# Decode attention, two heads at a time: 48 KB rows for K and V, p.V for 8 keys of two heads per weight load, q as rows on three partitions

## The chip, the cores and the metric

The kernel runs on one core of one Trainium2 chip (trn2). The metric is the device time of one execution in microseconds (us); the profile's span is some 2 us shorter than the time of the same execution. A program on one core has no second core to compare with, so "fast" here means no run more than 1.5% above the fastest of its kernel.

## The reference

Four attention layers in a row, A, B, A, B, each with its own K and V caches and its own two projections, for one token of width 640. A layer appears twice, so its caches are read twice.

```python
# x: (1, 1, 640); per layer: k_cache, v_cache (1, 32, 8192, 192), wq (640, 6144), wo (6144, 640), all bf16
def layer(x, k_cache, v_cache, wq, wo):             # heads 32, head width 192
    q = layernorm(x) @ wq                           # -> 32 heads x 192
    p = softmax(einsum("qd,kd->qk", q, k) * 192 ** -0.5)
    return x + concat(einsum("qk,kd->qd", p, v)) @ wo
x = layer(x, A...); x = layer(x, B...); x = layer(x, A...); x = layer(x, B...)
```

One caution on correctness. With these inputs a layer adds so little to x that the comparison with the reference cannot see it. So no run here says anything about the numerical result of the attention, nor about the "mended head mapping" that is part of the change; where a recorded text calls a result right, that means that the program makes every sum, not that it was checked.

## The kernel before

K and V of a head come as one load of 3 MB each into one of eight slots: 128 partitions with 64 keys each, a row of 24,576 bytes per partition. A slot is loaded again when its reader has freed it. Six head tiles (K 0 and V 0 of layer A, V 28 to 31 of layer B) stay on chip for the layer's second pass.

```python
NSLOT = 8
KEPT = {0: {("k", 0), ("v", 0)}, 1: {("v", 28), ("v", 29), ("v", 30), ("v", 31)}}
...
# one load: free = the events that freed what the slot held
f = lambda s: s.dma_start(t, w[n[0]][0, head(*n[1:])].rearrange("(p j) d -> p (j d)", p=P))
return SP.op(f, *free, sem=semS[i], inc=16)
```

Scores: the vector engine (DVE) multiplies K by q in four chunks in place, the tensor engine (PE) sums over the head width with an identity as held weights. When PE is through, the K slot is free.

```python
def products(h):
    for c in range(4):
        e = DV.op(lambda v, d0=d0: v.tensor_tensor(k3[:, :, d0:d0 + QD], kin[:, :, d0:d0 + QD],
                  q_sb[qi][:, d0:d0 + QD].unsqueeze(1).broadcast_to([P, J, QD]), ALU.mult))
    ...                                            # 24 matmuls of 512 columns, identity held
    freed[nt] = ev_S[h] = e
```

p.V: two keys per partition are the weights (2 columns), their V rows (2 x 192 columns) stream. Of the 2 x 2 blocks of the result only the diagonal ones are wanted. ScalarE (ACT) scales and copies the result, and two small matmuls pick the two diagonal blocks and sum over partitions. There are two result banks, O0 and O1, used in turn.

```python
def values(h):
    for m in range(J // 2):                        # 32 matmuls, each with its own weight load
        OB[par][32 * g:32 * g + 2, 0:2 * DH] += p_sb[pi][:, j:j + 2].T @ t[:, j * DH:(j + 2) * DH]
    freed[nv_] = e
    AC.op(lambda a: a.activation(o_sb, OB[par], ACT.Copy, scale=rl[pi]))
def gather(h):
    for i in range(2):                             # PE
        TB[0:1, C_O:C_O + DH] += pick[:, i:i + 1].T @ o_sb[:, i * DH:(i + 1) * DH]
```

(The updates in the last two excerpts are written shorter than in the program.)

Of the kernel before, what the change touches and what calls it, by code (L numbers as in the profile page):

```python
# [11 lines left out]
class Queue:  # L12
# [18 lines left out]
    def op(self, fn, *events, sem=None, inc=1, signal=True, bank=None):  # L31

        if bank is not None:
            self.wait(*[ev for q, ev in bank.items() if q is not self])
        self.wait(*events)
        if not signal:
            self.items.append((fn, None, 0))
            return None
        sem = self.sem if sem is None else sem
        self.counts[id(sem)] = self.counts.get(id(sem), 0) + inc  # L40
        self.items.append((fn, sem, inc))
        if bank is not None:
            bank[self] = (sem, self.counts[id(sem)])
        return sem, self.counts[id(sem)]
# [11 lines left out]
def matmul_held(t, out, lhsT, rhs, start, stop):  # L56

    return t.add_instruction(mybir.InstMatmult(  # L58
        name=t.bass.get_next_instruction_name(), engine=mybir.EngineType.PE,
        ins=[t.lower_ap(rhs), t.lower_ap(lhsT, for_matmul_weights=True)], outs=[t.lower_ap(out)],  # L60
        start_tensor_calc=start, stop_tensor_calc=stop, tile_size=(128, 128), tile_position=(0, 0), ldweights=False))


HEADS_W = 10
Q_FIRST = 2
O_LAST = 2
NSLOT = 8
AHEAD = 4
KEPT = {0: {("k", 0), ("v", 0)}, 1: {("v", 28), ("v", 29), ("v", 30), ("v", 31)}}


def build(nc, A_x, A_k, A_v, A_wq, A_wo, B_x, B_k, B_v, B_wq, B_wo, out):
# [3 lines left out]
    J = SK // P  # L76
    DC = D // P
    EPS = 1e-5
    NL = 4
    QD = DH // 4  # L80
    R = 512 // J
    W = [dict(k=A_k, v=A_v, wq=A_wq, wo=A_wo), dict(k=B_k, v=B_v, wq=B_wq, wo=B_wo)]
    NW = HEADS_W * DH // P
    QC = (H - Q_FIRST) * DH
    TS = J * DH
    QW = H * DH
    Q_PARTS = [[(0, 2), (2, 2), (4, 1)] if l < 2 else [(0, 1), (1, 2), (3, 2)] for l in range(NL)]
    O_PART = [P] * NL
    OI = [O_LAST * DH // n for n in O_PART]
    NB = 3  # L90
    G = 4
    FORWARD = dict(heads=list(range(H)), q0=0, q1=Q_FIRST * DH, wo=[0, HEADS_W, 2 * HEADS_W], wol=H - O_LAST)
    BACKWARD = dict(heads=[H - 2, H - 1] + list(range(H - HEADS_W, H - 2)) + list(range(O_LAST, H - HEADS_W))
                    + list(range(O_LAST)), q0=(H - Q_FIRST) * DH, q1=0,
                    wo=[H - HEADS_W, O_LAST, O_LAST + HEADS_W], wol=0)
    ORDER = [FORWARD, FORWARD, FORWARD, BACKWARD]

    with ExitStack() as ctx:
# [3 lines left out]
        def ps(name):  # L102
            return ctx.enter_context(nc.psum_tensor(name, [P, 512], F32))
# [7 lines left out]
        wq0 = [sb(f"wq0{i}", [P, DC, Q_FIRST * DH], BF16) for i in range(2)]  # L111
        orow = sb("orow", [1, HEADS_W * DH], BF16)
        oT = sb("oT", [P, NW], BF16)
        oTl = sb("oTl", [P, max(OI)], BF16)
        o_sb = sb("o_sb", [P, 2 * DH], F32)
        q_sb = [sb(f"q_sb{i}", [P, DH], BF16) for i in range(3)]
        qT = sb("qT", [P, H * DH // P], BF16)
        ones = sb("ones", [P, 1], F32)
        small = sb("small", [P, 48], F32)
# [6 lines left out]
        pick = col(2)  # L126
        one_b = sb("one_b", [1, 1], BF16)
        neghalf = col(1)
        s_sb = [sb(f"s_sb{i}", [P, J], F32) for i in range(2)]
        p_sb = [sb(f"p_sb{i}", [P, J], BF16) for i in range(AHEAD)]  # L130
        m_bf = [sb(f"m_bf{i}", [P, 1], BF16) for i in range(2)]
        negm = [col(1) for i in range(2)]
        l_col = [col(1) for i in range(2)]
        rl = [col(1) for i in range(AHEAD)]
# [14 lines left out]
        OB = [ps("O0"), ps("O1")]  # L149
        QT = ps("QT")  # L150
        TB = ps("TB")
        YB = ps("YB")
        use = {b: {} for b in ("QM", "S0", "S1", "O0", "O1", "QT", "TB", "YB")}
# [18 lines left out]
        e = PO.op(lambda g: g.memset(pick[:], 0.0))  # L172
        for t in range(G):
            for i in range(2):
                e = PO.op(lambda g, t=t, i=i: g.affine_select(
                    out=pick[:, i:i + 1], in_=pick[:, i:i + 1], compare_op=ALU.not_equal, fill=1.0,
                    base=-(32 * t + i), pattern=[[0, 1]], channel_multiplier=1), e)
        ev_const = PO.op(lambda g: g.memset(neghalf[:], -0.5))
        for b in OB:
            ev_zero = DV.op(lambda v, b=b: v.memset(b[:], 0.0), bank=use["O0" if b is OB[0] else "O1"])  # L180


        def head(l, p):
            return ORDER[l]["heads"][p]

        def first_load(kind, l, p):

            n = (kind, head(l, p))
            if l >= 2 and n in KEPT[l - 2]:
                return (kind, l - 2, ORDER[l - 2]["heads"].index(n[1]))  # L190
            return (kind, l, p)

        def stays(kind, l, p):
            return l < 2 and (kind, head(l, p)) in KEPT[l]

        steps, plan = [], []
        for l in range(NL):
# [6 lines left out]
            else:  # L204
                plan.append(("wq", l, 0))
                steps.append(("wq", l, 0))
            for p in range(H):
                if p in (HEADS_W, 2 * HEADS_W):
                    b = p // HEADS_W - 1
                    steps += [("wc", l, b), ("wo", l, b)]  # L210
                    plan.append(("wo", l, b))
                if first_load("k", l, p) == ("k", l, p):
                    plan.append(("k", l, p))
                if stays("k", l, p):
                    plan.append(("t", l, p))
                if l == 2 and p == 0:
                    part = [("m", l, 0), ("wq", l, 1), ("s", l, 0), ("v", l, 0), ("wq", l, 2)]
                elif p < H - AHEAD:
                    part = [("m", l, p), ("s", l, p), ("v", l, p)]
                else:  # L220
                    part = [("m", l, p)]
                    if p > H - AHEAD:
                        part.append(("s", l, p - 1))
                    if p == H - 1:
                        part.append(("s", l, p))
                        part += [("v", l, i) for i in range(H - AHEAD, H)]
                        part.insert(-O_LAST, ("wc", l, 2))
                steps += part
                plan += [n for n in part if n[0] == "v" and first_load(*n) == n]
                if l == 3 and p == 1:  # L230
                    for g in (1, 2):
                        plan.append(("wq", l, g))
                        steps.append(("wq", l, g))
            plan.append(("wo", l, 2))
            steps.append(("wo", l, 2))
            plan.append(("wol", l))
            steps.append(("wol", l))
# [3 lines left out]
        def released(n):  # L241

            if n[0] in "kvt":
                l, p = n[1:]
                if n[0] != "t" and stays(*n):
                    l, p = n[1] + 2, ORDER[n[1] + 2]["heads"].index(head(*n[1:]))
                return at[("v" if n[0] == "v" else "m", l, p)]
# [4 lines left out]
        def allot(n):  # L252

            ns = [("wq", n[1], g) for g in range(3)] if n[0] == "wq" and n[1] < 2 else [n]
            end = [-1 if h is None else released(h) for h in holder]
            first = -1 if n[1] == 0 and n[0] in "kv" and stays(*n) else 1
            i = min(range(NSLOT - len(ns) + 1), key=lambda i: (max(end[i:i + len(ns)]), first * i))
            for j, m in enumerate(ns):
                place[m] = i + j
                before[m] = [h for h in holder[i:i + len(ns)] if h is not None]  # L260
# [24 lines left out]
        def wol_rows(l):  # L285
# [5 lines left out]
            return pool[0:O_PART[l], i:i + OI[l] * D]  # L291

        def transfer(n):
# [4 lines left out]
            if n[0] == "wol":  # L298
                r0 = o["wol"] * DH
                if O_PART[l] == P:  # L300
                    return SP.op(lambda s: s.dma_start(
                        wol_rows(l), w["wo"][r0:r0 + O_LAST * DH].rearrange("(p i) n -> p (i n)", p=P)),
                        *free, sem=semOL, inc=16)
                k = O_PART[l] // O_LAST
                for h in range(O_LAST):
                    e = SP.op(lambda s, h=h: s.dma_start(
                        wol_rows(l)[h * k:(h + 1) * k],
                        w["wo"][r0 + h * DH:r0 + (h + 1) * DH].rearrange("(q e i) n -> e q (i n)", e=8, i=OI[l])),
                        *free, sem=semOL, inc=16)
                return e  # L310
            if n[0] == "t":
                return max(free, key=lambda e: e[1]) if free else None
            if n[0] == "wob":
                r0 = o["wo"][2] * DH
                return SP.op(lambda s: s.dma_start(
                    slot[place[("wo", l, 2)]][:, (NW - NB) * D:NW * D],
                    w["wo"][r0:r0 + HEADS_W * DH].rearrange("(p i) n -> p (i n)", p=P)[:, (NW - NB) * D:]),
# [3 lines left out]
            if n[0] in "kv":  # L321
                f = lambda s: s.dma_start(t, w[n[0]][0, head(*n[1:])].rearrange("(p j) d -> p (j d)", p=P))
            elif n[0] == "wq" and l < 2:
                f = lambda s: s.dma_start(pool[:, i * TS:i * TS + DC * QW], w["wq"].rearrange("(p c) n -> p (c n)", c=DC))
            elif n[0] == "wq":
# [3 lines left out]
                    w["wq"][:, o["q1"]:o["q1"] + QC].rearrange("(p c) n -> p c n", c=DC)[:, c0:c0 + k, :])  # L329
            else:  # L330
                r0 = o["wo"][n[2]] * DH
                k = NW - NB if n == ("wo", NL - 1, 2) else NW
                f = lambda s: s.dma_start(
                    t[:, 0:k * D], w["wo"][r0:r0 + HEADS_W * DH].rearrange("(p i) n -> p (i n)", p=P)[:, 0:k * D])
# [10 lines left out]
        def ahead():  # L345

            while issued[0] < len(plan):
                m = plan[issued[0]]
                if any(b not in freed for b in before[m]):
# [4 lines left out]

        last = dict(q=[None] * 3, s=[None, None], p=[None] * AHEAD, m=[None, None], negm=[None, None],
                    lc=[None, None], rl=[None] * AHEAD, S=[None, None], O=[ev_zero, ev_zero], L=[None, None],
                    osb=None, orowb=None)
# [339 lines left out]
```

## Time and profile before

| | before |
|---|---|
| time, median of 3 | 1996.76 us (1996.27 to 1997.4) |
| bytes read | 848.36 MB |
| share of the load queue | 99.4% of 16 engines' span |
| PE, DVE, ACT busy | 70%, 53%, 11% |

From the page of the kernel before: the busy line; the line of what the loads moved in each fortieth of the span; the queue line (packets, MB, share of the 16 DMA engines' span); and the chain that ended last, by engine.

```profile
PE 1392.6 (70%) x10438; PEld 318.0 (16%) x7494; DVE 1047.4 (53%) x1074; ACT 220.3 (11%) x665; POOL 4.5 (0%) x22
...
GB/s 410 431 431 428 432 429 429 430 431 430 428 430 431 428 432 428 431 429 429 431 382 431 428 431 428 431 430 429 431 429 427 430 430 429 430 429 429 429 432 345
...
q1 hardware_dynamic: 40256, 848.38, 99.4%
...
DMA 65%; PE 21%; DVE 12%; ACT 1%; issue 1%; another core or an unknown queue 0%; DVEq 0%
```

The reader sees a kernel bound by its loads: the rate stays at 427 to 432 GB/s but for three places. They are the start (slice 1), the passage from the second layer to the third (slice 21), and the end (slice 40).

How soon a K slot comes free, from the chain: K of a head has landed at 88.79, DVE multiplies it, PE sums it, and the next K load is issued at 97.09, 8.3 us after the landing.

```profile
88.79 6.78 DVE pool L495 x4
95.61 1.46 PE S L58 x6
97.09 35.51 DMA pool<-in_A_k_cache_dram
```

The passage, closer, in the table of stretches (columns: stretch, its length, busy time and instructions of each engine, granted PE clock, DMA share, GB/s):

```profile
core 0: us, PE busy (x) PEld busy (x) DVE busy (x) ACT busy (x) POOL busy (x), PEclk, DMA share, GB/s
...
1010.00:1030.00 20.00, 15.22 (x250) 9.85 (x242) 5.71 (x13) 3.14 (x9) 0.54 (x1) 0.76 0.77 315
```

The tail in the timeline (start, duration, engine, line, operation): p.V of the last head starts when its V has landed; one ACT copy, a small matmul and the output projection follow.

```profile
1983.22 2.73 PE L546 MATMUL O<-pool,p_sb 128*2 128x384 bf16 x32 [1.41 <-DMA pool<-in_B_v_cache_dram]
...
1986.00 0.94 ACT L561 ACTIVATE o_sb<-O,small 128x192 f32<-128x192 f32 x2 [3.99 <-PE O L546]
...
1987.00 0.86 PE L585 MATMUL TB<-small,o_sb 128*64 128x1 f32 x12 [1.05 <-ACT o_sb L561]
...
1987.79 2.56 PE L465 MATMUL YB<-oT,pool 128*128 128x1 bf16 x60
```

And the groups (busy us, mean ns; then idle before them) of the work that the change touches:

```profile
L546 PE MATMUL O<-pool,p_sb 128*2 128x384 bf16 x4096 | 346.5, 420 | 1.4 <-DMA pool<-in_B_v_cache_dram 1.4
...
L546 PEld LDWEIGHTS O<-pool,p_sb 128*2 128x2 bf16 x4096 | 128.0, 88 | 134.8 <-issue 98.4
...
L561 ACT ACTIVATE o_sb<-O,small 128x384 f32<-128x384 f32 (+1 forms) x136 | 77.2, 579 | 233.2 <-PE O L546 233.2
```

The trace also records each DMA packet. Here and below I sum the load queue's packets of over 600 bytes: their number, their time divided by 16 (how long the engines would be busy if they shared the work evenly), and what is left of the stretch from the first packet to the last as idle. This is my own arithmetic on those records, not a view of the profile. For the kernel before: start 1.7 us, packets 1980.2 us, idle 7.8 us, and 5.0 us from the last packet to the span's end; together 1994.7 us, the span.

### The profile page before, as it was taken

To read this page: it belongs to the slowest core of one execution; us is meant where nothing else is said; L and a number is where in the kernel's file an instruction comes from. 1 tells how busy PE (TensorE), PEld (TensorE's weight loads), DVE (VectorE), ACT (ScalarE), POOL (GpSimd) and SP (SyncE) were. 2 spreads that over 40 slices of the span, in tenths; PEclk is the share of its full clock that TensorE was granted. 3 is DMA by queue.
4 is the path that set the end of the run, shared out by engine and by line. 5 is a ranking of instruction groups with operands and counts; after the bars stand their busy time and mean duration, and the time that the engine had idled before them with its cause. 6 is when DMAs were issued, how large, how long until landed. Compare 5 with 4: busy or idle time off the path is not lost.

```text
span 1994.7 us, 20412 instructions
## 1 busy us (share of the span) xinstructions
PE 1392.6 (70%) x10438; PEld 318.0 (16%) x7494; DVE 1047.4 (53%) x1074; ACT 220.3 (11%) x665; POOL 4.5 (0%) x22
## 2 busy tenths in 40 slices
PE   4777777667567766767777676777776768767766
PEld 1111111111311111211031111111112212111112
DVE  3554554556255455455726545545663465554563
ACT  0111111110111111111011111111101111111111
POOL 0000000000000000000000000000000000000000
PEclk9888888887688888788878878887897888987889
DMA  9999999999999999999999999999999999999998
GB/s 410 431 431 428 432 429 429 430 431 430 428 430 431 428 432 428 431 429 429 431 382 431 428 431 428 431 430 429 431 429 427 430 430 429 430 429 429 429 432 345
DMA packets 40487, 849.67 MB, mean 426 GB/s; under 512 B 4688, under 2 KB 4688, under 8 KB 5328
## 3 DMA queue, kind: packets, MB, share of 16 engines
q1 hardware_dynamic: 40256, 848.38, 99.4%
q8 instruction: 70, 1.15, 0.2%
q14 instruction: 17, 0.14, 0.0%
q10 hardware_dynamic: 144, 0.00, 0.0%
HBM read 848.36 MB, written 0.00 MB: 425 GB/s over the span
## 4 chain that ended last, share of the span: by engine, by line
DMA 65%; PE 21%; DVE 12%; ACT 1%; issue 1%; another core or an unknown queue 0%; DVEq 0%
DMA pool<-in_B_k_cache_dram 32%; DMA pool<-in_A_k_cache_dram 30%; PE S L58 13%; DVE pool L495 10%; PE O L546 3%; DMA pool<-in_B_wo_dram 2%; PE TB L569 1%; DMA x_bf<-in_A_x_dram 1%; PE S L508 1%; PE YB L465 1%; DVE s_sb L516 1%; ACT p_sb L526 1%; PE QT L427 1%; PE TB L530 1%; DVE small L523 0%
## 5 line engine op out<-in xcount | busy, mean ns | idle before, releaser
L495 DVE TENSOR_TENSOR pool<-pool,q_sb 128x3072 bf16<-128x3072 bf16 x512 | 865.5, 1752 | 406.4 <-DMA pool<-in_A_k_cache_dram 208.3
L58 PE MATMUL S<-pool,ident 128*128 128x512 bf16 x2944 | 797.2, 425 | 35.1 <-DVE pool L495 34.9
L546 PE MATMUL O<-pool,p_sb 128*2 128x384 bf16 x4096 | 346.5, 420 | 1.4 <-DMA pool<-in_B_v_cache_dram 1.4
L508 PE MATMUL S<-pool,ident 128*128 128x512 bf16 x128 | 60.4, 472 | 225.7 <-DVE pool L495 225.5
L516 DVE TENSOR_REDUCE s_sb<-S 128x64 f32<-128x512 f32 x128 | 88.3, 690 | 229.1 <-PE S L58 229.1
L546 PEld LDWEIGHTS O<-pool,p_sb 128*2 128x2 bf16 x4096 | 128.0, 88 | 134.8 <-issue 98.4
L569 PE MATMUL TB<-o_sb,small 128*1 128x192 f32 x480 | 122.8, 389 | 38.2 <-DVE small L534 27.1
L453 ACT ACTIVATE q_sb<-QM 128x192 bf16<-128x192 f32 x120 | 39.6, 330 | 961.2 <-PE QM L446 961.2
L446 PEld LDWEIGHTS QM<-ident,qT 128*128 128x128 bf16 x240 | 23.1, 98 | 741.0 <-issue 725.6
L530 PE MATMUL TB<-small,ones 128*128 128x1 f32 x256 | 49.7, 263 | 109.9 <-ACT p_sb L526 109.9
L520 PE MATMUL QM<-ident,m_bf 128*128 128x128 bf16 x128 | 27.8, 217 | 122.9 <-DVE m_bf L519 121.2
L561 ACT ACTIVATE o_sb<-O,small 128x384 f32<-128x384 f32 (+1 forms) x136 | 77.2, 579 | 233.2 <-PE O L546 233.2
L534 DVE RECIPROCAL small<-TB 128x1 f32<-128x1 f32 x128 | 21.5, 168 | 122.4 <-PE TB L530 122.4
L526 ACT ACTIVATE p_sb<-s_sb,small 128x64 bf16<-128x64 f32 x128 | 44.5, 348 | 266.5 <-DVE small L523 266.5
L523 DVE TENSOR_REDUCE small<-QM 128x1 f32<-128x128 f32 x128 | 37.3, 291 | 62.3 <-PE QM L520 62.3
L575 ACT ACTIVATE orow<-TB 1x192 bf16<-1x192 f32 x120 | 38.3, 319 | 200.7 <-PE TB L569 200.7
L530 PEld LDWEIGHTS TB<-small,ones 128*128 128x128 f32 x256 | 38.9, 191 | 130.4 <-ACT p_sb L526 130.4
L508 PEld LDWEIGHTS S<-pool,ident 128*128 128x128 bf16 x128 | 12.7, 99 | 285.8 <-DVE pool L495 285.8
L520 PEld LDWEIGHTS QM<-ident,m_bf 128*128 128x128 bf16 x128 | 12.3, 96 | 215.3 <-ACT q_sb L453 126.9
L569 PEld LDWEIGHTS TB<-o_sb,small 128*1 128x1 f32 x480 | 33.5, 89 | 81.1 <-DVE small L534 36.0
L465 PE MATMUL YB<-oT,pool 128*128 128x1 bf16 x900 | 38.0, 178 | 5.1 <-DMA pool<-in_A_wo_dram 2.3
L465 PEld LDWEIGHTS YB<-oT,pool 128*128 128x128 bf16 x900 | 37.0, 131 | 5.9 <-ACT oT L479 2.9
(50 smaller groups left out, 215.4 us busy)
## 6 DMA issues: line engine op xcount, KB each, us to landing
pool<-in_B_k_cache_dram SPq DMA_DIRECT2D x64, 3072.0 KB, 35.5
pool<-in_A_k_cache_dram SPq DMA_DIRECT2D x63, 3072.0 KB, 27.6
pool<-in_A_v_cache_dram SPq DMA_DIRECT2D x63, 3072.0 KB, 33.3
pool<-in_B_v_cache_dram SPq DMA_DIRECT2D x60, 3072.0 KB, 37.2
pool<-in_A_wo_dram SPq DMA_DIRECT2D x6, 2400.0 KB, 24.0
pool<-in_B_wo_dram SPq DMA_DIRECT2D x5, 2400.0 KB, 33.3
pool<-in_A_wq_dram SPq DMA_DIRECT2D x1, 7680.0 KB, 20.8
pool<-in_B_wq_dram SPq DMA_DIRECT2D x1, 7680.0 KB, 29.3
```

The costliest lines, as they stand in the source:

```text
L58: return t.add_instruction(mybir.InstMatmult(name=t.bass.get_next_instruction_name(), engine=mybir.EngineType.PE, ins=[t.lower_ap(rhs), t. ...
L453: lambda a: a.activation(q_sb[i][:], QM[:, 0:DH], ACT.Copy), e, last["q"][i], bank=use["QM"])
L465: e = PE.op(lambda t, i=i, c=c, f=y_first[0], fin=end and i == k - 1: t.matmul(YB[:, c:c + 1], lhsT=t3[:, i, c:D:DC], rhs=o[:, i:i + 1], s ...
L495: e = DV.op(lambda v, d0=d0: v.tensor_tensor(k3[:, :, d0:d0 + QD], kin[:, :, d0:d0 + QD], q_sb[qi][:, d0:d0 + QD].unsqueeze(1).broadcast_t ...
L508: t.matmul(S[:, :], lhsT=ident[:], rhs=k3[:, :, d0:d0 + R], start=True, stop=fin) if d0 == 0 else
L516: ev_s = DV.op(lambda v: v.tensor_reduce(s_sb[par][:], S[:].rearrange("p (j r) -> p j r", r=R), AX.X, ALU.add), ev_S[h], last["s"][par], b ...
L520: e = PE.op(lambda t: t.matmul(QM[:, C_MX:C_MX + P], lhsT=m_bf[par][:, 0:1].broadcast_to([P, P]), rhs=ident[:], start=True, stop=True), ev ...
L526: ev_p[h] = AC.op(lambda a: a.activation(p_sb[pi][:], s_sb[par][:], ACT.Exp, bias=negm[par][:, 0:1], accum_out=l_col[par][:]), ev_n, ev_s, ...
L530: e = PE.op(lambda t: t.matmul(TB[:, C_L + par:C_L + par + 1], lhsT=ones[:, 0:1].broadcast_to([P, P]), rhs=l_col[par][:], start=True, stop ...
L546: e = PE.op(lambda e, g=g, j=j, f=m < G, fin=fin: e.matmul(OB[par][32 * g:32 * g + 2, 0:2 * DH], lhsT=p_sb[pi][:, j:j + 2], rhs=t[:, j * D ...
L561: ev_os[h] = AC.op(lambda a, o=o, i=i: a.activation(o, i, ACT.Copy, scale=rl[pi][:, 0:1]), e, ev_rl[h], last["osb"], bank=use[f"O{par}"])
L569: e = PE.op(lambda t, i=i: t.matmul(TB[0:1, C_O:C_O + DH], lhsT=pick[:, i:i + 1], rhs=o_sb[:, i * DH:(i + 1) * DH], start=(i == 0), stop=( ...
```

## The change

Its intent: two heads share the 128 partitions (64 each, with 128 keys per partition), so K and V of a pair come as one load of 6 MB with rows of 49,152 bytes: half as many packets. (That holds for 102 of the 125 pair loads; the others stay two loads of 24 KB rows, see `whole` below.) p.V takes 8 keys at once, two heads in 16 weight columns, with three streams of 512 columns on the same weights: a quarter of the weight loads. q is computed as three rows that stream wq, not as columns that load it as weights. And the output rows of the last layer, which runs its heads in another order, are written where wo expects them.

The core of the diff, cut (the p.V loop, the old q line and the new one are written shorter than they are):

```diff
-HEADS_W = 10
+PAIRS_W = 5
-KEPT = {0: {("k", 0), ("v", 0)}, 1: {("v", 28), ("v", 29), ("v", 30), ("v", 31)}}
+KEPT = {0: {("k", 0)}, 1: {("v", 14), ("v", 15)}}
+    VK = 8
...
+        def whole(kind, l, p):                     # one load of 48 KB rows into two slots, or two halves
+            if kind == "t":
+                return False
+            if kind == "k":
+                return l < 2 or l == 3 and p > 1
+            if p == NPAIR - 1:
+                return False
+            return l != 2 or p not in (PAIRS_W, 2 * PAIRS_W)
...
-                f = lambda s: s.dma_start(t, w[n[0]][0, head(*n[1:])].rearrange("(p j) d -> p (j d)", p=P))
+                r = w[n[0]][0, h:h + 2].rearrange("h (p j) d -> (h p) (j d)", j=J)
+                if whole(*n[:3]):
+                    f = lambda s: s.dma_start(pool[:, i * TS:(i + 2) * TS], r)
+                else:
+                    f = lambda s: s.dma_start(t, r[:, n[3] * TS:(n[3] + 1) * TS])
...
-                for m in range(J // 2):            # p.V: 2 keys, 384 columns, 32 weight loads a head
+                for r in range(rounds):            # 8 keys x 2 heads = 16 weight columns
+                    for c in range(3):             # 3 x 512 columns; weights loaded for c == 0, held after
+                        for g in range(G): ...
-                    ev_os[h] = AC.op(lambda a, o=o, i=i: a.activation(o, i, ACT.Copy, scale=rl[pi][:, 0:1]), ...
+                for i in range(VK):                # the gather: eight DVE passes pick the diagonal blocks
+                    e = DV.op(lambda v, i=i: (
+                        v.tensor_scalar(acc[:], O[:, 0:DH], pick[:, 0:1], None, ALU.mult) if i == 0 else
+                        v.scalar_tensor_tensor(out=acc[:], in0=O[:, i * DH:(i + 1) * DH], scalar=pick[:, i:i + 1],
+                                               in1=acc[:], op0=ALU.mult, op1=ALU.add)), ...)
...
-                QT[:, b:b + 1] = t3[:, c, b * P:(b + 1) * P].T @ xb      # q: 225 matmuls a layer
+                OY[32 * r:32 * r + 1, b * 512:b * 512 + w] = xb.T @ t3   # q: 60 matmuls a layer, three rows
...
-                o0 = (h % HEADS_W) * DH
+                o0 = (pair(l, p) - ORDER[l]["wo"][p // PAIRS_W]) * PD
```

The p.V result is now 1536 columns wide, three banks, so there is one of it and not two. And the steps of a pair stand in this order: score half 0 of pair p (its products and sums for the first 64 of the 128 keys per partition), the gather of pair p - 1, score half 1 of pair p, softmax, p.V. The gathers of pairs 4 and 9 and of the last two do not wait for a next pair; behind those of 4, 9 and 14 come the "columns", small matmuls that turn the output rows into columns for wo.

## The prediction

> **What bounds the kernel now.** The loads. The page's queue part puts the load queue at 99.4% of the sixteen engines' span; it moves 848 MB, and the slice line holds 428 to 432 GB/s except in the first slice (410), the middle one (382) and the last (345). PE is busy 70%, DVE 53%. In the chain of waits DMA is 65%. At 430 GB/s the bytes alone take about 1975 us; the other 20 us are the start (about 2), the change from the second to the third layer (about 5: 308 and 321 GB/s from 1010 to 1030 us) and the tail (about 12 from the last V landing to the end).
>
> **What the change does to them.**
>
> 1. Bytes: the same. Six head-tiles stay on chip before, three pair-tiles (six heads) after.
>
> 2. Rate. The trace's packet records show one packet per row: median 915 ns for 24,576 B, 433 ns for 11,520 B, 2268 ns for 61,440 B. That is 8 to 12 ns on top of the bytes at 435 GB/s, the ceiling that the Trainium skill gives ("DMA: Bandwidth & Descriptors", Where 436 GB/s comes from). So a 49,152-byte row should take about 1817 ns, against 2 x 915. 102 of the 125 pair loads are whole (48 KB rows): 13,056 fewer packets x 13 ns / 16 engines = -10.6 us. Fewer load completions and instruction fetches: -1 to -1.5.
>
> 3. Off the path: p.V goes from 64 matmuls of 384 columns with 64 weight loads per pair to 48 of 512 with 16; q goes from 225 weight-load-bound matmuls per layer to 60 streaming ones. Added: eight DVE passes over 192 columns per pair, about 2.6 us (estimate from the 291 ns reduction over 128), with DVE near 19 of the 29 us that a pair's loads take. None of it binds in steady state.
>
> 4. Coarser slots cost something. Third layer's start: the first V load now needs two slots, so it waits for both halves of the kept K pair: two times 6.8 us of DVE plus 1.5 of PE and about 1 from issue to data, where before one head sufficed. The loads in front (13.7 us) run out about 6 us earlier: +6. In layers one and two, K of pairs 5 and 10 waits for the K pair just before it, and only 5.7 us of output weights cover it: 0 to 1 us each, +2 in all. The tail's gather is longer by about 0.7. Resynchronised engines: +1.
>
> 5. The mended mapping costs no time.
>
> Sum: 1996.8 - 12 + 6 + 2 + 0.7 + 1 = about 1994.5.
>
> **Predicted: 1994 us, 8 in 10 between 1985 and 2003.** Faster by over 2%: 0.01; within 2%: 0.97; slower by over 2%: 0.02.
>
> **What would show it.** Step 2: load packets near 25,500, 49,152-byte ones near 1817 ns, steady slices at 431 to 433 GB/s. Step 4: a dip of 8 to 11 us of lost loading at the third layer's start, SP waiting there on PE's score matmuls; small dips at pairs 5 and 10 of the first two layers. Step 3: PE busy and weight loads down, DVE busy up by about 130 us, no new steady wait.
>
> **What would make it wrong.** 48 KB strides that HBM serves otherwise than interpolated; less slack than the 7 us I count with two pair buffers in the third layer; row-group matmuls that do not overlap (+3 us at the start).

## The result

| | before | after |
|---|---|---|
| time, median of 4 runs each | 1997.0 us (1996.27 to 1997.4) | 2018.03 us (2016.4 to 2018.68) |
| ratio | | 1.0104, 95% interval 1.0087 to 1.0122 |
| packets / 16, from the records | 1980.2 us | 1973.5 us |
| loads idle between first and last packet | 7.8 us | 28.0 us |
| last packet to the end of the span | 5.0 us | 12.4 us |
| span of the profiled run | 1994.7 us | 2015.6 us |

The last three rows come from the profiled run of each kernel, one run each. Ratios are the mean time of one kernel's fast runs over that of the other's of the same rounds, so not quite the ratio of the medians.

The three rows account for the whole difference: -6.7 us of packets, +20.2 us of idle loads, +7.4 us of tail make +20.9 us. (Packets overlap a little on an engine, so their sum is somewhat too large and the idle time too small: with loads alone, below, the sum exceeds the stretch by 3.8 us with 24 KB rows and by 1.3 us with 48 KB rows.) The page after:

```profile
PE 1278.0 (63%) x8246; PEld 146.2 (7%) x3074; DVE 1210.3 (60%) x1395; ACT 139.5 (7%) x461; POOL 4.4 (0%) x22
...
GB/s 418 429 432 418 427 437 410 436 436 424 436 430 436 414 433 427 402 428 436 428 311 435 427 430 434 428 381 432 433 421 429 435 427 433 436 427 434 434 432 295
...
q1 hardware_dynamic: 25568, 848.38, 98.0%
...
DMA 56%; DVE 24%; PE 18%; ACT 1%; issue 1%; SPq 0%
```

PE and its weight loads fell as intended (PEld 318.0 to 146.2 us), packets fell from 40,256 to 25,568, and the load queue's share fell too, from 99.4 to 98.0%. In the chain that ended last DVE rose from 12 to 24%. The slices show where loading stopped: slice 21 (311), slice 27 (381), slice 40 (295), and less so slices 4, 7, 14 and 17 (418, 410, 414, 402), in which K of pairs 5 and 10 of the first two layers is loaded. The groups:

```profile
L617 DVE SCALAR_TENSOR_TENSOR acc<-OY,small,acc 128x192 f32<-128x192 f32 x448 | 187.2, 418 | 15.7
...
L590 PEld LDWEIGHTS OY<-pool,p_sb 128*16 128x16 bf16 x1024 | 30.1, 104 | 269.1 <-issue 176.1
...
L616 DVE TENSOR_SCALAR acc<-OY,small 128x192 f32<-128x192 f32 x64 | 26.7, 417 | 1.9
```

So the eight passes take 187.2 + 26.7 = 213.9 us in all, 3.3 us per pair.

Where the loads stood idle, from the packet records (us lost, averaged over the 16 engines; places under 0.5 us left out; because of the overlap the sum can differ from the idle time above by about 1 us):

| place | before | after |
|---|---|---|
| before K of pairs 5 and 10, layers one and two (four places) | 0 | 7.5 (1.3, 1.3, 1.6, 3.3) |
| third layer: wq waits until the last output projection frees its slot | 4.6 | 8.0 |
| third layer: first V waits for the kept K pair | 0 | 5.0 |
| third layer: V of pair 10 | 0 | 5.1 |
| last loads | 4.1 | 2.5 |

Four of these places in the stretches after (the line at 165 is K of pair 5 in layer one):

```profile
core 0: us, PE busy (x) PEld busy (x) DVE busy (x) ACT busy (x) POOL busy (x), PEclk, DMA share, GB/s
165.00:175.00 10.00, 6.42 (x30) 0.31 (x5) 7.79 (x8) 1.93 (x7) 0.00 (x0) 1.00 0.89 349
...
1020.00:1030.00 10.00, 5.72 (x114) 5.22 (x108) 3.84 (x14) 0.27 (x1) 0.00 (x0) 0.67 0.25 85
...
1040.00:1050.00 10.00, 9.70 (x77) 0.45 (x13) 7.25 (x7) 0.21 (x1) 0.00 (x0) 1.00 0.65 251
1345.00:1355.00 10.00, 9.61 (x104) 3.96 (x89) 6.88 (x5) 0.19 (x1) 0.00 (x0) 0.51 0.80 342
```

The first place in the timeline: K of pair 4 has landed at 153.7; its first half is multiplied, then come the gather's passes, then the second half; only when PE has summed it (last group of matmuls at 171.03) does the sync engine's queue issue the next K load, at 172.56, 18.9 us after the landing. In between the queue had V of pair 4 (its rows began between 151.5 and 165.9) and the output weights (through on the slowest engine at 173.5), some 20 us of loads in all; the first row of the next K began at 173.5. I call the loads that stand between a K pair and the load that needs its slots the cover.

```profile
153.71 6.77 DVE L530 TENSOR_TENSOR pool<-pool,q_sb 128x3072 bf16<-128x3072 bf16 x4 [6.85 <-DMA pool<-in_A_k_cache_dram]
...
160.72 0.42 DVE L616 TENSOR_SCALAR acc<-OY,small 128x192 f32<-128x192 f32 x1
161.17 3.13 DVE L617 SCALAR_TENSOR_TENSOR acc<-OY,small,acc 128x192 f32<-128x192 f32 x7
164.22 6.75 DVE L530 TENSOR_TENSOR pool<-pool,q_sb 128x3072 bf16<-128x3072 bf16 x4
...
171.03 1.46 PE L58 MATMUL S<-pool,ident 128*128 128x512 bf16 x6 [0.21 <-DVE pool L530]
...
172.56 0.33 SPq L356 DMA_DIRECT2D pool<-in_A_k_cache_dram  x1
```

And the tail after. The gather of pair 14 ends at 1995.87 (1992.74 + 3.13); behind it the program has PE do the columns of the output; p.V of the last pair starts at 1998.73 (the granted clock was 0.57 while it ran, and 0.51 during the last p.V of the kernel before), and then the last gather takes 3.6 us, where the kernel before had one ACT copy of 0.94 us.

```profile
1992.74 3.13 DVE L617 SCALAR_TENSOR_TENSOR acc<-OY,small,acc 128x192 f32<-128x192 f32 x7
...
1997.72 1.07 PE L512 MATMUL TB<-one_b,rows 1*128 1x1 bf16 x15 [0.81 <-ACT rows L639]
...
1998.73 0.60 PE L590 MATMUL OY<-pool,p_sb 128*16 128x512 bf16 x4
...
2004.05 0.40 DVE L616 TENSOR_SCALAR acc<-OY,small 128x192 f32<-128x192 f32 x1
2004.49 3.13 DVE L617 SCALAR_TENSOR_TENSOR acc<-OY,small,acc 128x192 f32<-128x192 f32 x7
...
2007.68 1.04 PE L624 MATMUL TB<-small,acc 128*64 128x1 f32 x12 [3.76 <-DVE acc L617]
```

### The profile page after: what moved, and what is told of

Read it like the earlier page. It is cut to its first block, busy times and chain, and to the rows that moved or that the text cites. A ratio compares the mean times of both kernels' runs of the same rounds, so it can differ in the third digit from the quotient of the medians.

```text
span 2015.6 us, 13729 instructions
## 1 busy us (share of the span) xinstructions
PE 1278.0 (63%) x8246; PEld 146.2 (7%) x3074; DVE 1210.3 (60%) x1395; ACT 139.5 (7%) x461; POOL 4.4 (0%) x22
## 3 DMA queue, kind: packets, MB, share of 16 engines
q1 hardware_dynamic: 25568, 848.38, 98.0%
HBM read 848.36 MB, written 0.00 MB: 421 GB/s over the span
## 4 chain that ended last, share of the span: by engine, by line
DMA 56%; DVE 24%; PE 18%; ACT 1%; issue 1%; SPq 0%
DMA pool<-in_A_k_cache_dram 27%; DMA pool<-in_B_k_cache_dram 27%; DVE pool L530 17%; PE S L58 11%; DVE acc L617 4%; PE OY L58 3%; PE OY L590 2%; DMA pool<-in_B_wq_dram 1%; DMA pool<-in_A_v_cache_dram 1%; PE S L543 1%; ACT p_sb L567 1%; PE OY L501 1%; DVE s_sb L552 1%; DVE acc L616 1%; PE TB L628 0%
## 5 line engine op out<-in xcount | busy, mean ns | idle before, releaser
L58 PE MATMUL S<-pool,ident 128*128 128x512 bf16 x2944 | 825.9, 440 | 21.4 <-DVE pool L530 20.9
L543 PE MATMUL S<-pool,ident 128*128 128x512 bf16 x128 | 66.4, 518 | 367.7 <-DVE pool L530 367.5
L58 PE MATMUL OY<-pool,p_sb 128*16 128x512 bf16 x2048 | 202.2, 479 | 0.0
L617 DVE SCALAR_TENSOR_TENSOR acc<-OY,small,acc 128x192 f32<-128x192 f32 x448 | 187.2, 418 | 15.7
L590 PE MATMUL OY<-pool,p_sb 128*16 128x512 bf16 x1024 | 124.8, 475 | 101.5 <-ACT p_sb L567 63.3
L628 PE MATMUL TB<-acc,small 128*1 128x192 f32 x240 | 56.4, 363 | 120.2 <-DVE acc L617 120.2
L639 ACT ACTIVATE rows<-TB,small 1x192 bf16<-1x192 f32 x120 | 43.2, 405 | 1044.2 <-PE TB L628 1044.2
L567 ACT ACTIVATE p_sb<-s_sb,small 64x128 bf16<-64x128 f32 x128 | 55.7, 435 | 155.8 <-DVE small L561 155.0
L628 PEld LDWEIGHTS TB<-acc,small 128*1 128x1 f32 x240 | 16.1, 86 | 479.9 <-DVE acc L617 467.7
L590 PEld LDWEIGHTS OY<-pool,p_sb 128*16 128x16 bf16 x1024 | 30.1, 104 | 269.1 <-issue 176.1
L501 PE MATMUL OY<-oT,pool 128*128 128x1 bf16 x900 | 38.1, 178 | 2.2 <-ACT oT L515 2.2
L501 PEld LDWEIGHTS OY<-oT,pool 128*128 128x128 bf16 x900 | 37.0, 131 | 2.9 <-ACT oT L515 2.9
L616 DVE TENSOR_SCALAR acc<-OY,small 128x192 f32<-128x192 f32 x64 | 26.7, 417 | 1.9
```

Source lines behind the costliest of these rows:

```text
L58: return t.add_instruction(mybir.InstMatmult(name=t.bass.get_next_instruction_name(), engine=mybir.EngineType.PE, ins=[t.lower_ap(rhs), t. ...
L501: e = PE.op(lambda t, i=i, c=c, f=y_first[0], fin=end and i == k - 1: t.matmul(YB[:, c:c + 1], lhsT=t3[:, i, c:D:DC], rhs=o[:, i:i + 1], s ...
L543: t.matmul(S[:, :], lhsT=ident[:], rhs=k3[:, :, d0:d0 + R], start=True, stop=fin) if d0 == 0 else
L567: ev_p[p] = AC.op(lambda a, h=h, r=r: a.activation(p_sb[par][r, :, h], s[r, :], ACT.Exp, bias=negm[par][r, 0:1], accum_out=l_col[par][r, h ...
L590: t.matmul(o, lhsT=x, rhs=y, start=f, stop=fin) if c == 0 else
L616: v.tensor_scalar(acc[:], O[:, 0:DH], pick[:, 0:1], None, ALU.mult) if i == 0 else
```

## The experiments

Theory: 48 KB rows do save the packet time that was predicted, but the eight DVE passes and the coarser slots let the loads run dry. Rivals: 48 KB rows are themselves worse when they stream; the place of the passes, not their amount, is what counts; the pair structure costs something else. One more rival needs no run of its own: PE's granted clock was lower in the changed kernel (0.795 in the profiled run, 0.841 before). But the runs below with one pass and with two had 0.786 and 0.792, and were as fast as the kernel before or within 2 us of it; so the lower clock is not what costs.

### Loads alone, 24 KB rows against 48 KB rows

Edit: everything but the loads taken out; 124 pairs' K and V, four pair buffers in turn, each load waiting only for the one that had its buffer before. The output is x.

```diff
+        for n in range(124):
+            if WHOLE: ev = dma_start(pool[:, 2 * i * TS:(2 * i + 2) * TS], two heads)     # 49,152-byte rows
+            else:     for u in range(2): dma_start(pool slot 2 * i + u, one head)          # 24,576-byte rows
```

24 KB rows, expected:

> Loads alone, one head per load, 24,576-byte rows, 248 loads; the output is wrong on purpose. Both theories use this as the base: 31,744 row packets of about 915 ns over 16 engines are 1815 us; I expect 1815 to 1825 us.

48 KB rows, expected:

> The same bytes, loads alone, a pair of heads per load, 49,152-byte rows; wrong on purpose. Theory 1 (48 KB rows are really quicker, the loss is idle time of the loads): about 1818 ns a packet, 10 to 13 us less than the run with 24 KB rows (0.6 to 0.7%). Rival (48 KB rows are served worse once they stream): no gain or a loss.

Measured: 1821.3 us and 1811.56 us (2 runs each, agreeing within 0.4 us). The page's packet line for the first, then for the second (the packets include one small one per load and engine):

```profile
DMA packets 36002, 780.18 MB, mean 429 GB/s; under 512 B 4256, under 2 KB 4256, under 8 KB 4256
```

```profile
DMA packets 18145, 780.16 MB, mean 431 GB/s; under 512 B 2272, under 2 KB 2272, under 8 KB 2272
```

A 24,576-byte packet took 916 ns, a 49,152-byte one 1820 ns. 48 KB rows are 9.7 us or 0.53% faster for the same bytes, just under what was expected. (By the sum of packets / 16 it is 12.0 us, 1817.4 against 1805.4; the 24 KB packets overlapped more.) The rival that they stream worse is out.

### Every row as two halves

```diff
         def whole(kind, l, p):
+            return False
```

> The changed kernel with every 48 KB row loaded as two halves of 24 KB (two loads of 3 MB), each half issued when its own slot is free. Theory 1: the packets cost 6 to 10 us more, the 7 us of idle loads at pairs 5 and 10 of the first two layers go, the wait at the third layer's start and the tail stay: 2013 to 2020 us. Rival (48 KB rows are what costs): 2000 us or less. Steady slices at 428 to 430 GB/s.

Measured: 2008.95 us, ratio 1.0059 (1.0044 to 1.0074): 9 us less than the changed kernel, though its packets are the small ones again (packets/16 1981.2 us, +7.7). Idle fell from 28.0 to 16.1 us: the four places at pairs 5 and 10 are gone, as expected, and the projection wait at the third layer fell from 8.0 to 4.2. The tail fell from 12.4 to 8.5 us, which I had not expected; it and the projection wait make the miss. A likely reason is that DVE gets the first half of the last K pairs 7 us earlier; that was not tested by itself. The run is also less clean than its edit looks: K halves are now given slots one by one, and the program's own plan puts 185 of 277 tiles elsewhere. One effect shows: the halves of the kept K pair lie in swapped slots, so the first V of the third layer still waits for the later half, and its 5 us of idle stay. The rival (48 KB rows are what costs) wanted 2000 us or less.

### Halves in five places only

```diff
-                return l < 2 or l == 3 and p > 1
+                return l < 2 and p not in (PAIRS_W, 2 * PAIRS_W) or l == 3 and p > 1
-            return l != 2 or p not in (PAIRS_W, 2 * PAIRS_W)
+            return l != 2 or p not in (0, PAIRS_W, 2 * PAIRS_W)
```

> The changed kernel with halves in five places only: K of pairs 5 and 10 in layers one and two, and the first V of the third layer. Theory 1: the idle at those four K loads (7.4 us) and most of the 5 us before the first V of the third layer go: 2018 - 12 = 2004 to 2009 us. Rival (the eight DVE passes and the p.V order bind throughout): no more than 3 us gained.

Measured: 2003.12 us, ratio 1.0028 (1.0011 to 1.0045), 15 us less than the changed kernel and just under the stated range. The four places and the wait before the first V of the third layer are gone from the packet records. The projection wait rose from 8.0 to 10.1 us: the loads come to it earlier and the projection does not. The tail stayed at 12.6 us. So where the loads ran dry a release was late; 48 KB rows elsewhere did no harm.

### The order of steps at a layer's end

```diff
-  score half 1 of pair 15, p.V 14, softmax 15, gather 14, columns, p.V 15, gather 15
+  p.V 14, score half 1 of pair 15, gather 14, softmax 15, p.V 15, columns, gather 15
```

> The changed kernel; only the order of six steps at each layer's end: p.V of pair 14 ahead of the second score half of pair 15, its gather ahead of the last softmax, and the columns of the output behind p.V of pair 15. Theory (the longer tail and the late output projection at the layer's end come from one p.V buffer and PE held up behind the gather of pair 14): 3 to 5 us less tail and about 4 us less idle at the third layer's start, 2018 - 8 = 2008 to 2013 us. Rival (only the DVE time of the gather counts there, order is indifferent): within 2 us of 2018.

Measured: 2017.29 us, ratio 1.01 (1.0084 to 1.0115): nothing gained, so by its time this run speaks for the rival. Its trace says otherwise: the tail fell from 12.4 to 8.4 us and the projection wait from 8.0 to 3.7 us, both as the theory had it, but a new idle stretch of 6.3 us stood at the end of the third layer. There V of pair 15 goes into the slots of K of pair 15, and PE, now waiting for V of pair 14 first, frees them late. The sync queue's pair of V loads took 19.47 us to issue, and PE stood still for 9.55 us before p.V of pair 14:

```profile
1495.73 19.47 SPq L364 DMA_DIRECT2D pool<-in_A_v_cache_dram  x2
...
1505.24 0.60 PE L596 MATMUL OY<-pool,p_sb 128*16 128x512 bf16 x4 [9.55 <-DMA pool<-in_A_v_cache_dram]
```

Idle rose by 2.2 us in all and the tail fell by 4.0. What one release gained, another lost: the reason was right and the remedy too wide.

### One DVE pass of eight

```diff
-                for i in range(VK):
+                for i in range(1):                  # a wrong sum on purpose
```

> The changed kernel with one of the eight DVE passes of each gather (a wrong sum on purpose): 3.1 us less DVE per pair. Theory (the gather sits in the chain before K of pairs 5 and 10 in layers one and two, and twice at each layer's end): those four idles of 1.3 to 3.1 us go, the third layer's start and the tail lose 3 to 6 us each: 2000 to 2007 us. Rival (the gather is off the path, as the prediction had it): 2015 us or more.

Measured: 1994.05 us, ratio 0.9983 (0.9967 to 1.0): 24 us less than the changed kernel, more than expected. Idle fell from 28.0 to 14.8 us (the four places gone, the projection wait 8.0 to 2.5), the tail from 12.4 to 5.3 us. The first V of the third layer and V of pair 10 kept their waits (5.4 us each). The passes were on the path wherever the loads had little cover. In its slices 4, 7, 14, 17 and 21 stand 432, 427, 435, 425 and 354 GB/s, where the changed kernel had 418, 410, 414, 402 and 311:

```profile
GB/s 410 434 432 432 432 432 427 437 429 429 434 435 429 430 431 433 425 433 431 430 354 431 428 432 429 432 385 426 434 429 427 436 428 438 428 436 431 429 436 362
```

### The gather behind both score halves

```diff
-                if late is not None:
-                    steps.append(("e", l, late)); late = None
                 steps.append(("m", l, p, 1))
+                if late is not None:
+                    steps.append(("e", l, late)); late = None
```

> The changed kernel; the gather of the last pair stands behind both score halves on DVE instead of between them, nothing else. If the place of the eight passes matters (they hold back the release of K): the four idles before K of pairs 5 and 10 in layers one and two go, the layer ends stay as they are: 2008 to 2013 us. If their amount matters wherever they stand: 2016 us or more.

Measured: 2006.18 us, ratio 1.0048 (1.0033 to 1.0063), 12 us less with not one pass fewer (DVE busy 1207.0 us against 1210.3), and 2 us below the stated range, since the layers' ends did gain a little. The four places are gone; the projection wait fell to 6.8 and the tail to 11.3 us. The first place in the timeline of this run: both halves are multiplied in one go, PE's last sums follow, and the next K load is issued 15.0 us after K landed and not 18.9; the passes run beside it.

```profile
154.10 13.44 DVE L530 TENSOR_TENSOR pool<-pool,q_sb 128x3072 bf16<-128x3072 bf16 x8 [9.70 <-DMA pool<-in_A_k_cache_dram]
...
167.60 1.46 PE L58 MATMUL S<-pool,ident 128*128 128x512 bf16 x6 [0.21 <-DVE pool L530]
...
168.24 3.14 DVE L617 SCALAR_TENSOR_TENSOR acc<-OY,small,acc 128x192 f32<-128x192 f32 x7
...
169.13 0.33 SPq L356 DMA_DIRECT2D pool<-in_A_k_cache_dram  x1
```

So about half of what the passes cost is their place between the two halves; the other half, at the layers' ends, is their length.

### Two keys per weight load: the p.V part undone alone

```diff
-    VK = 8
+    VK = 2            # 64 matmuls of 384 columns a pair with 64 weight loads; two DVE passes a gather
```

> The changed kernel with the p.V part undone alone: 2 keys per weight load, so 64 matmuls of 384 columns and two DVE passes in each gather instead of eight; a right result. Theory (the passes are what the change lost its time to; the saved weight loads were worth nothing): 1995 to 2001 us, as with one pass, less than the run before by 17 us or more. Rival (the gain of the one-pass run came from something else, such as skipped waits): 2010 us or more. PE weight loads rise back to about 4,096 for p.V.

Measured: 1998.32 us, ratio 1.0011 (0.9996 to 1.0026): 20 us less than the changed kernel. Its page:

```profile
PE 1248.7 (63%) x9270; PEld 228.3 (11%) x6146; DVE 1049.9 (53%) x1011; ACT 139.5 (7%) x461; POOL 4.4 (0%) x22
...
GB/s 412 437 428 431 432 432 424 435 432 428 435 430 435 420 435 430 426 432 435 427 364 434 426 430 432 427 382 432 441 424 425 439 426 434 432 431 433 430 435 349
```

Weight loads rose from 3074 to 6146 instructions and PEld from 146.2 to 228.3 us, and the kernel got faster. On balance the p.V part cost 20 us. The saved weight loads were worth little or nothing: seven passes fewer gave 24 us, so six fewer should give about 20.6 (an estimate, if each pass costs the same), and this run, which gives up the saving as well, gained 19.7. What is left against the kernel before: packets -7.5 us, idle +8.1 us (of which the first V of the third layer 4.5 and V of pair 10 4.8), tail +0.5 us.

### Towards a better version

First the halves in five places, the step order in all layers, and, in the third layer, the first K half of pair 11 loaded ahead of V of pair 10:

```diff
+        i = plan.index(("v", 2, 2 * PAIRS_W, 0))
+        plan[i:i + 3] = [plan[i + 2], plan[i], plan[i + 1]]
```

> The halves in five places, the step order, and in the third layer the first K half of pair 11 loaded ahead of V of pair 10 (so V waits behind 14.6 us of loads, not 7.3). Theory: the 4.3 to 5 us idle before V of pair 10 goes as well: 2003 - 4 - 8 = 1991 us, 1987 to 1995, below the kernel before. Rival (order is indifferent): 1998 to 2000 us.

Measured: 1999.53 us, ratio 1.0011 (0.9996 to 1.0026), outside what was expected. The wait before V of pair 10 is gone, but the new one at the third layer's end is there (6.1 us), as in the run with the step order alone. The next one keeps the step order to layers two and four and takes 2 keys per weight load:

```diff
-        for l in range(NL):     # the step order at a layer's end
+        for l in (1, 3):
-    VK = 8
+    VK = 2
```

> 48 KB rows with the halves in five places, K of pair 11 ahead of V of pair 10 in the third layer, the step order at the end of layers two and four only (in the third layer it delayed V of pair 15 by 5.6 us), and 2 keys per weight load. Theory: idle loads at or under the 7.8 us of before, packets 7 to 9 us less, tail about 5 us: 1984 to 1990 us, under the kernel before. Rival (something else in the pair structure costs): 1995 us or more.

Measured: 1988.45 us, ratio 0.996 (0.9943 to 0.9977): below the kernel before, by 0.4%. Packets 1970.9 us (-9.3 against before), idle 7.1 us (before 7.8), tail 5.3 us (before 5.0). Slice 21 is at 393 GB/s (before 382, after 311), slice 27 at 430 (after 381):

```profile
GB/s 412 438 431 429 434 433 431 429 434 428 433 434 431 432 434 430 430 434 432 428 393 436 427 429 432 429 430 427 432 431 426 436 430 435 432 429 431 435 431 352
```

Last, the same with K of pairs 5 and 10 whole again:

> The same with K of pairs 5 and 10 in layers one and two loaded whole again. Theory (with two passes K is released in time): equal to the run before it within 1.5 us. If not: some 5 us more, idle at those four loads.

Measured: 1988.19 us, ratio 0.9962 (0.9947 to 0.9977), the same. The four places show 0 to 0.8 us of idle each, in a profiled run that was the slowest of the four (1992.05 us; the others took 1987.4 to 1988.85). With two passes the whole K pair is released just in time.

## Why the prediction was wrong

The prediction said 1994 us, 1985 to 2003; the result was 2018. Its class, within 2%, held. Point by point:

1. Bytes equal: right (848.36 MB read in both).
2. Rate: right in mechanism. The prediction said 1817 ns for a 49,152-byte packet and about 25,500 packets; measured 1818 ns (median) and 25,568. The size was off: of the term of -12 us, -10.6 were packets, and packets / 16 measured -6.7 us in this kernel, -12.0 with loads alone (which have more packets to save). In this kernel the mean packet (1825 ns) lies above its median; that the packets at the edge of an idle stretch are drawn out is likely (the mean is 1821 ns in the 1988.45 us run, which has 7.1 us of idle), but was not separated. The Trainium skill's page "DMA: Bandwidth & Descriptors" (Where 436 GB/s comes from) gives 435 GB/s as the ceiling of the ports into the on-chip memory; loads alone in 48 KB rows keep 429 to 435 GB/s between the first slice and the last, so the trace agrees. The same section says that for loads from HBM some 358 GB/s bind; here, with one core at work, they did not.
3. "Eight DVE passes over 192 columns per pair, about 2.6 us ... None of it binds in steady state": this is the step that failed. Taken word for word it held: between the places in the table no idle stretch above 0.5 us shows. But the step was headed "Off the path" and put nothing into the sum, and off the path the passes were not. Their size was low (3.6 us from the first pass to the last, 3.3 us of busy time), but the argument was worse than the number. It compared DVE's sum, 19 of 29 us per pair, with the load time, and asked nothing about the order: in 12 of 16 pairs the passes stand before the second half of a K pair, so K's release came 3.6 us later, and where the cover was only that pair's V and the 5.7 us of output weights the loads ran dry. At the layers' ends they stand in the chain twice. Experiments: with one pass -24 us, with two passes (all sums made) -20 us, with the passes moved -12 us. With one pass, so with passes nearly as free as the step had them, the rest of the sum comes out: packets -8.4, idle +7.0, tail +0.3 us against the kernel before, -1.1 us where the sum said -2.3. That its single terms were off by up to 4 us and made up for one another is luck.
4. Coarser slots. "+6" for the first V of the third layer: 5.0 us, right. "+2" for K of pairs 5 and 10: 7.5 us, because each place lost 1.3 to 3.3 us and not 0 to 1; the five-place experiment removed them. "The tail's gather is longer by about 0.7": the tail grew by 7.4 us, and 7.1 of it went with seven of the passes. Not in the sum, though "less slack ... in the third layer" stood among the risks: V of pair 10 in the third layer (5.1 us), a slot wait behind one 3 MB half (7.3 us of loads) where the first half of K of pair 10 needs 9.8 us from its first multiplication to the issue of V (1347.60 to 1357.40 in the timeline), and the landing and the start of the transfer come on top. And the projection wait, +3.4 us, which the gather lengthened (2.5 us with one pass).
5. "The mended mapping costs no time": not tested by any run. Nor was q as rows tested by itself.

So what made the prediction wrong is what step 3 and the tail term left out: with two passes (1998.3 us) the time would have been inside the stated range.

The Trainium skill's page "Perfetto Trace Analysis" (DMA Optimizations) gives both halves: larger DMAs use the memory's bandwidth better (its examples are of a few KB), and splitting a DMA may let some of the work start sooner (it has idle DMA engines in mind). Here the first was worth 9.7 us by itself (24 to 48 KB rows) and the second, in five places, 15 us, though the changed kernel's queue was 98% busy. The same page (Optimizing Scalar/DVE Operations) says that each DVE instruction has a fixed access cost, larger for PSUM, and that larger operations can help when the engine is saturated. The passes, 418 ns each for 192 columns, are small instructions, but DVE was 60% busy and not saturated, and no run here separates the fixed part.

## What to carry to other kernels

In a kernel bound by loads, work on another engine is free only while it delays no release of a buffer; take each load's slot, go to the step that frees it, and compare the time from landing to release with the loads that stand in between, before adding anything in front of that step. Fewer weight loads on an engine with slack buy nothing, so do not pay for them with passes on the engine that frees the buffers. When a unit of loading is doubled, keep it in halves where the cover is thin, and use the large unit where the queue is deep.

## What the Trainium skill lacked or had wrong

- "VectorE: DVE Perf Modes" (the errata section's table) gives 120 + FD cycles at 0.96 GHz for an operation from PSUM, FD being the columns: an estimate of 325 ns for 192 fp32 columns. The passes here, PSUM and SBUF in and SBUF out with a per-partition scalar, took 417 and 418 ns each (mean), and 3.58 us for eight in a row (160.72 to 164.30). The page notes itself that its row for SBUF is too low for a single operation; for the PSUM row it has no such note.
- "DMA: Bandwidth & Descriptors" (Why small descriptors are slow) puts about 3 cycles of overhead on a packet and calls it a matter of small descriptors. Loads alone show that rows as large as 24 KB still gain from doubling: 916 against 1820 ns, so 12 ns per packet saved, and 0.53% of the time.
- No page gives a figure for how far the 16 engines drift apart within one queue. In the kernel before, some engines had begun the 3,840-byte packets of the last output weights at 1009.1 us, while others moved 19,200-byte packets of the load in front of it until 1017.4 us; the matmuls that read that load began at 1017.86 us, after the slowest engine.
